# Attention interleaved with a squared-ReLU layer: batch 1's projection, its attention steps and the copy of V moved in the schedule, one more square on ScalarE

## Chip, cores, metric

The kernel runs on one core of one Trainium2 chip. The metric is device time in microseconds, the median of several executions of the whole kernel; lower is better. "Batch 0", "batch 1" and so on are the eight items of the batch; the change's "second batch" is batch 1.

TensorE is PE in the profile, its weight loads PEld, VectorE is DVE, ScalarE is ACT, GpSimd is POOL, SyncE is SP. A profile line names what an instruction writes and, after the arrow, what it reads: Q_sb, K_sb and V_sb are the loaded inputs, ps_kv the projection, qT and kT the transposed Q and K, vp the projected V, ps_att what attention computes on TensorE, h_relu and hsq the relu and its square. L462 is line 462 of the run's own kernel, so one instruction can have different lines in two kernels.

## The reference, cut

```python
# q, k, v: (8 batches, 8 heads, 1024 rows, 64); E, F: (64, 1024); w_in: (512, 2048); w_out: (2048, 512)
k_proj = einsum('ks,bhsd->bhkd', E, k)          # 64 projected rows per head
v_proj = einsum('ks,bhsd->bhkd', F, v)
attn   = softmax(q @ k_proj^T / 8)              # only 64 columns
x      = (attn @ v_proj) reordered to (8192, 512)
h      = maximum(x @ w_in, 0)
out    = (h * h) @ w_out
```

## The kernel before

The squared-ReLU layers keep TensorE busy. While batch b runs through them, the attention of batch b+1 is put between their matmuls. A batch's layers are a list of small steps: 16 steps of the first layer and 15 of the second, for each of two chunks (in batch 0 both first layers come before both second layers). The second layer is computed from sums and differences of blocks, tiles s (of the squares) and T (of the weights), which VectorE makes; its results are ps_x, ps_y and ps_z. Tables say which attention call comes before which step. On TensorE, VectorE and ScalarE the instructions keep the order in which the Python code emits them; on SyncE and GpSimd, which issue the DMAs, the framework chooses the order itself.

```python
def project(self):                    # 16 matmuls: K to the lower 64 partitions, V to the upper
    ps = self.ps["kv"] = ffn_psum("ps_kv")
    ...
def copy_kp(self):
    ...
    nc.vector.tensor_copy(self.kp[:, :, 0, :], ps_k)
    nc.vector.tensor_copy(self.kp[:, :, 1, :], self.kp[:, :, 0, :])
    nc.sync.dma_start_transpose(out=self.kT[:], in_=self.kp[:]...)          # K's transpose
def transpose_q(self):
    nc.sync.dma_start_transpose(out=self.qT[:], in_=self.Q[:]...)           # Q's transpose
def copy_vp(self):
    ...
    for e in range(2):
        nc.scalar.copy(self.vp[KP:P, :, e], ps_v[:, :, e])
    nc.vector.tensor_copy(self.vp[0:KP], self.vp[KP:P])                     # down to the lower partitions

BATCH_1 = {                            # calls for batch 1, between the steps of batch 0
    33: "project", 34: "copy_kp, copy_vp, transpose_q",
    45: "scores 0, scores 1, exponentials 0", 46: "exponentials 1", ... }
BATCH_2 = {**PIECES, 1: "", 2: "", 9: "project", 10: "copy_kp", 11: "copy_vp"}   # batch 2, in batch 1
ON_SCALAR = {(0, 1): (2, 4, 6), (1, 0): (4,)}    # (batch, chunk): which squares run on ScalarE

def square(k, n, ps):                  # after each first-layer step; two steps make one square
    nc.scalar.activation(r[:, n], ps[:], AF.Relu)
    ...                                # k in ON_SCALAR: nc.scalar.activation(o, r[:], AF.Square)
    nc.vector.tensor_tensor(out=o, in0=r[:], in1=r[:], op=ALU.mult)
```

Q, K and V of a batch are loaded by GpSimd into single buffers, in the order Q, K, V from batch 2 on. The load of batch 2's Q needs the buffer that batch 1's Q leaves when its transpose has been done; K and V are queued behind it.

The softmax here doesn't subtract the row's maximum and nothing guards it: scores larger than these inputs give would overflow.

Of the kernel before, what the change touches and what calls it, by code (L numbers as in the profile page):

```python
# [17 lines left out]
def kernel(  # L18
# [137 lines left out]
    class Attention:  # L156
# [30 lines left out]
        def copy_vp(self):  # L187
            self.vp = proj_pool.tile([P, H, 2, D // 2], BF16, name="vp")
            ps = self.ps["kv"]
            ps_v = ps[KP:P, :].rearrange("k (h d e) -> k h e d", h=H, e=2)  # L190
            for e in range(2):
                nc.scalar.copy(self.vp[KP:P, :, e], ps_v[:, :, e])
            nc.vector.tensor_copy(self.vp[0:KP], self.vp[KP:P])

        def scores(self, pr):
# [204 lines left out]


    PIECES = {
        0: "transpose_q", 1: "copy_kp", 2: "copy_vp",
        24: "scores 0, scores 1, exponentials 0", 25: "exponentials 1",
        27: "sums 0, values 0 0, reciprocals 0", 30: "values 0 1", 31: "normalize 0 0", 32: "normalize 0 1",
        47: "scores 2, scores 3, exponentials 2", 48: "exponentials 3",
        50: "sums 1, values 1 0, reciprocals 1", 53: "values 1 1", 54: "normalize 1 0", 55: "normalize 1 1",
    }
    BATCH_1 = {
        33: "project", 34: "copy_kp, copy_vp, transpose_q",  # L410
        45: "scores 0, scores 1, exponentials 0", 46: "exponentials 1",
        48: "sums 0, values 0 0, reciprocals 0", 51: "values 0 1, normalize 0 0", 52: "normalize 0 1",
        53: "scores 2, scores 3, exponentials 2", 54: "exponentials 3",
        56: "sums 1, values 1 0, reciprocals 1", 59: "values 1 1, normalize 1 0", 60: "normalize 1 1",
    }

    BATCH_2 = {**PIECES, 1: "", 2: "", 9: "project", 10: "copy_kp", 11: "copy_vp"}
    SECOND_HALF = {
        1: "last_of_first", 6: "second_half 0", 8: "second_half 1", 11: "second_half 2",
        12: "second_half 3, second_half 4, second_half 5",  # L420
# [2 lines left out]
        25: "T1 0", 26: "T1 1", 28: "T2 0", 30: "T2 1", 34: "T3 0", 35: "T3 1", 38: "T4 0", 39: "T4 1",  # L423
    }

    ON_SCALAR = {(0, 1): (2, 4, 6), (1, 0): (4,)}

    OPERANDS = {
        17: (0, 0, 0), 18: (0, 0, 1), 19: (0, 1, 0), 20: (0, 1, 1), 21: (0, 3, 0), 23: (0, 3, 1),
# [4 lines left out]
    def calls(table, n):  # L434
        for c in filter(None, table.get(n, "").split(", ")):
            name, *args = c.split()
            yield name, [int(a) for a in args]

    def ffn_groups(b, xT):
# [28 lines left out]
        def chunk(ch):  # L468
# [17 lines left out]
            def square(k, n, ps):  # L486
# [8 lines left out]
                o = hsq[:, :, j, :] if h != h1 else hsq[:, h, j:j + 2, :]  # L495
                if k in ON_SCALAR.get((b, ch), ()):
                    nc.scalar.activation(o, r[:], AF.Square)
# [160 lines left out]
    with tc.manual_schedule(engines=ORDERED):  # L658
# [10 lines left out]
        for b in range(B):  # L669
            for n, g in enumerate(ffn_groups(b, cur.xT)):  # L670
# [7 lines left out]
                if nxt:  # L678
                    for name, args in calls((BATCH_1, BATCH_2, PIECES)[min(b, 2)], n):
                        getattr(nxt, name)(*args)  # L680
# [36 lines left out]
```

## Time and profile before

| | before |
|---|---|
| median of 3 runs | 488.95 us (488.53 to 489.87) |
| span of the profiled run | 487.1 us, granted clock 1.0 |
| TensorE busy | 472.4 us (97%) |
| projection of batch 1 and second layers of batch 0 | 31.44 us (52.93 to 84.37) |
| batch 1, first chunk | 30.91 us (84.37 to 115.28) |
| batch 2, first chunk, for comparison | 27.88 us, without a projection (1.85 us) |

The stretches are differences of start times in the timeline of TensorE; "second layers" means here from step 32 on, whether its first work is the projection or the layer.

From the profile's page, the engines' busy time and the chain that ended last (shares of the span):

```profile
PE 472.4 (97%) x3618; PEld 292.5 (60%) x3619; DVE 317.2 (65%) x383; ACT 259.9 (53%) x408; POOL 33.0 (7%) x45
...
PE 92%; DVE 3%; ACT 2%; DMA 2%; issue 0%; SPq 0%
```

TensorE is nearly always busy, and the chain runs through it. The Trainium skill ("Perfetto Trace Analysis", section Identifying the Most-Contended Engine) says that this busy time is a bad measure of how close a kernel is to its limit. So one looks for TensorE's waits, not at its share. Those of the stretch that the change touches (line, released by, us in total, times, longest):

```profile
PE ps_att L199 <- DMA kT<-kp: 1.2, 1, 1.2
PE ps_y L462 <- DVE hsq L499: 0.7, 1, 0.7
```

The first is the wait of batch 1's scores for the transposed K. SyncE's timeline (start, duration, line, tile) and the chain from 61 to 67 us show what stands before it:

```profile
57.73 4.94 SPq L167 DMA_TRANSPOSE qT<-Q_sb  x1
62.73 1.28 SPq L185 DMA_TRANSPOSE kT<-kp  x1
```

```profile
61.18 1.50 SPq L167
62.68 0.06 issue
62.73 3.96 DMA kT<-kp
66.69 0.04 issue
66.73 0.63 PE ps_att L199 x8
```

Q's transpose was issued first, the moment Q had landed (57.7), and kept SyncE for 4.94 us. K's transpose came after it and landed at 66.69; the scores started at 66.73. The second wait is that of the second layer for the last square of batch 1's first chunk. VectorE's timeline shows its work until then (in brackets: idle before, and what ended it; the sums on line 456 between the squares, about 0.7 us each, are left out):

```profile
98.11 0.29 DVE L193 COPY vp<-vp 64x512 bf16<-64x512 bf16 x1 [2.80 <-ACT vp L192]
98.73 1.23 DVE L499 TENSOR_TENSOR hsq<-h_relu 128x1024 bf16<-128x1024 f32 x1 [0.33 <-ACT h_relu L491]
100.48 1.22 DVE L499 TENSOR_TENSOR hsq<-h_relu 128x1024 bf16<-128x1024 f32 x1
102.21 1.22 DVE L499 TENSOR_TENSOR hsq<-h_relu 128x1024 bf16<-128x1024 f32 x1
```

### The profile page before, as it was taken

Reading aid. Unit: us, or ns where it says so; the run is one execution under the profiler, and the core shown is the slowest. Engines: PE = TensorE matmul, PEld = TensorE weight load, DVE = VectorE, ACT = ScalarE, POOL = GpSimd, SP = SyncE. Lnnn points to the kernel's source line nnn. Section 1 sums busy time; section 2 is a strip of 40 time slices with the busy share of each in tenths; the row PEclk is TensorE's granted clock in tenths of the full one; section 3 lists DMA queues with packets and bytes.
Section 4 is the critical chain, followed back from the end, with each engine's and each line's share of the span. In section 5 each row is a group of like instructions: output and inputs, shape, how many; then the busy total and the mean of one; then the engine's idle time right before and its main releaser. Section 6 shows DMA issues by size and latency. Waiting matters only on the chain.

```text
span 487.1 us, 8385 instructions
## 1 busy us (share of the span) xinstructions
PE 472.4 (97%) x3618; PEld 292.5 (60%) x3619; DVE 317.2 (65%) x383; ACT 259.9 (53%) x408; POOL 33.0 (7%) x45
## 2 busy tenths in 40 slices
PE   4899999999999999999999999999999999999997
PEld 2544667465574755757466664747557484666656
DVE  2459855565947569385665848567684856848383
ACT  1387544655727556355654467365572746635351
POOL 7330020100020000200010000200000000000000
PEclk9999999999999999999999999999999999999999
DMA  9999989996289224991149920794232102020202
GB/s 163 204 205 208 161 138 218 235 188 163 38 139 227 40 87 88 149 208 41 46 87 180 176 87 12 132 212 90 88 68 72 46 1 87 2 87 0 87 0 87
DMA packets 72485, 55.46 MB, mean 114 GB/s; under 512 B 33920, under 2 KB 64640, under 8 KB 72448
## 3 DMA queue, kind: packets, MB, share of 16 engines
q0 software_dynamic: 30320, 29.36, 38.3%
q1 hardware_dynamic: 42128, 25.56, 20.5%
q8 instruction: 28, 0.46, 0.4%
q14 instruction: 9, 0.07, 0.0%
HBM read 59.24 MB, written 16.78 MB: 156 GB/s over the span
## 4 chain that ended last, share of the span: by engine, by line
PE 92%; DVE 3%; ACT 2%; DMA 2%; issue 0%; SPq 0%
PE ps_h L442 43%; PE ps_y L462 23%; PE ps_z L462 11%; PE ps_x L462 5%; PE ps_kv L175 3%; PE ps_att L214 2%; PE ps_att L199 2%; DVE hsq L499 1%; DMA kT<-kp 1%; DMA e_f<-in_E_dram 1%; ACT h_relu L491 1%; PE ps_k L249 1%; PE ps_fill L341 0%; ACT expT L302 0%; DVE qT L287 0%
## 5 line engine op out<-in xcount | busy, mean ns | idle before, releaser
L442 PE MATMUL ps_h<-xT,w_in 128*128 128x512 bf16 x1024 | 224.8, 379 | 0.0
L499 DVE TENSOR_TENSOR hsq<-h_relu 128x1024 bf16<-128x1024 f32 x124 | 151.2, 1222 | 63.0 <-ACT h_relu L491 63.0
L491 ACT ACTIVATE h_relu<-ps_h 128x512 f32<-128x512 f32 x256 | 150.9, 597 | 65.5 <-PE ps_h L442 65.3
L442 PEld LDWEIGHTS <-w_in 128*128 128x128 bf16 x1024 | 99.6, 98 | 117.9 <-issue 2.0
L462 PEld LDWEIGHTS <-s 128*128 128x128 bf16 x1024 | 98.5, 98 | 19.5 <-issue 8.1
L462 PEld LDWEIGHTS <-hsq 128*128 128x128 bf16 x768 | 73.2, 98 | 19.9 <-DVE hsq L499 3.4
L462 PE MATMUL ps_y<-T,s 128*128 128x256 bf16 x512 | 62.2, 273 | 0.1
L568 DVE TENSOR_TENSOR o_sb<-ps_z,p_b 128x512 f32<-128x512 f32 x16 | 11.1, 692 | 53.5 <-issue 25.7
L456 DVE TENSOR_TENSOR s<-hsq 128x1024 bf16<-128x1024 bf16 x64 | 43.6, 684 | 0.0
L564 ACT COPY o_sb<-ps_y 128x512 f32<-128x512 f32 x15 | 8.8, 585 | 56.3 <-PE ps_y L462 56.1
L233 DVE TENSOR_TENSOR xT<-ps_att,rs 128x1024 bf16<-128x1024 f32 x28 | 33.0, 1217 | 6.9 <-ACT rs L227 6.9
L462 PE MATMUL ps_y<-w_out,hsq 128*128 128x256 bf16 x256 | 34.4, 273 | 0.7 <-DVE hsq L499 0.7
L462 PE MATMUL ps_x<-w_out,hsq 128*128 128x256 bf16 x256 | 33.2, 273 | 0.0
L462 PE MATMUL ps_y<-T,hsq 128*128 128x256 bf16 x256 | 31.6, 272 | 0.0
L462 PE MATMUL ps_z<-w_out,s 128*128 128x256 bf16 x256 | 30.8, 273 | 0.0
L462 PE MATMUL ps_z<-T,s 128*128 128x256 bf16 x256 | 30.7, 273 | 0.0
L206 ACT ACTIVATE expT<-ps_att 128x1024 bf16<-128x1024 f32 x28 | 27.2, 1028 | 5.4 <-PE ps_att L199 5.4
L564 ACT COPY p_b<-ps_y 128x512 f32<-128x512 f32 (+1 forms) x17 | 9.5, 560 | 27.9 <-PE ps_y L462 27.8
L78 POOL DMA_DIRECT2D Q_sb<-in_q_dram x7 | 6.1, 876 | 265.1 <-DMA qT<-Q_sb 264.7
L568 DVE TENSOR_TENSOR o_sb<-ps_y,p_d 128x512 f32<-128x512 f32 (+1 forms) x17 | 11.2, 660 | 18.5 <-PE ps_y L462 18.5
L456 DVE TENSOR_TENSOR s<-s,hsq 128x1024 bf16<-128x1024 bf16 x32 | 21.9, 687 | 0.5
L226 ACT ACTIVATE rs<-ps_att 128x1024 f32<-128x1024 f32 x14 | 14.3, 1023 | 14.7 <-PE ps_att L214 14.7
(73 smaller groups left out, 237.7 us busy)
## 6 DMA issues: line engine op xcount, KB each, us to landing
out_dram<-o_sb SPq DMA_DIRECT2D x30, 512.0 KB, 2.9
K_sb<-in_k_dram POOLq DMA_DIRECT2D x7, 1024.0 KB, 17.2
V_sb<-in_v_dram POOLq DMA_DIRECT2D x7, 1024.0 KB, 22.6
Q_sb<-in_q_dram POOLq DMA_DIRECT2D x7, 1024.0 KB, 10.0
w_in<-in_moe_w_in_dram POOLq DMA_DIRECT2D x8, 256.0 KB, 14.1
w_out<-in_moe_w_out_dram POOLq DMA_DIRECT2D x4, 512.0 KB, 14.4
K_sb<-in_k_dram POOLq DMA_DIRECT2D x2, 512.0 KB, 8.0
Q_sb<-in_q_dram POOLq DMA_DIRECT2D x2, 512.0 KB, 13.1
```

Source lines behind the costliest of these rows:

```text
L175: nc.tensor.matmul(ps[0:KP, :], lhsT=ET[:, i, :], rhs=kv[:, :, i, :], start=f, stop=l)
L199: nc.tensor.matmul(ps[o, bank, :], lhsT=self.kT[r, 2 * pr + j, :], start=True, stop=True, rhs=self.qT[r, NT * (2 * pr + j):NT * (2 * pr + ...
L206: nc.scalar.activation(e[:], self.ps["s", pr][:], AF.Exp, scale=SCALE)
L226: nc.scalar.activation(rs[:], self.ps["r", g][:], AF.Ln)
L233: nc.vector.tensor_tensor(out=self.xT[:, 2 * g + e].rearrange("p a n t -> p a (n t)"), in0=self.ps["v", g, e][:], in1=self.rs[g][:], op=AL ...
L442: nc.tensor.matmul(ps[:], lhsT=w_in_blk(cb, fb), rhs=xT[:, cb, :, 2 * ch:2 * ch + 2], start=(cb == 0), stop=(cb == NCB - 1),)
L456: nc.vector.tensor_tensor(out=s[o][:, js], in0=x, in1=y, op=op)
L462: nc.tensor.matmul(ps[tb] if len(ps) == 2 else ps[0][:, tb], lhsT=lhs[:, j, tb * P:(tb + 1) * P], rhs=rhs[:, j], start=first and n == 0 an ...
L491: nc.scalar.activation(r[:, n], ps[:], AF.Relu)
L499: multiply = lambda: nc.vector.tensor_tensor(out=o, in0=r[:], in1=r[:], op=ALU.mult)
L564: nc.scalar.copy(to[:, t], ps)
L568: nc.vector.tensor_tensor(out=to[:, t], in0=ps, in1=more[:, t], op=ALU.add)
```

## The change

Its intent: have batch 1's projected K copied and transposed sooner, ahead of Q; take the copy of V to the lower partitions out of VectorE's way; give ScalarE a second square in batch 1's first chunk. Batch 1's scores, exponentials, sums and values also move one step (about 0.87 us) later, the projection one step earlier; two of the four normalizations keep their step.

```diff
             for e in range(2):
                 nc.scalar.copy(self.vp[KP:P, :, e], ps_v[:, :, e])
+
+        def copy_v_down(self):
             nc.vector.tensor_copy(self.vp[0:KP], self.vp[KP:P])
 ...
-        0: "transpose_q", 1: "copy_kp", 2: "copy_vp",
+        0: "transpose_q", 1: "copy_kp", 2: "copy_vp", 4: "copy_v_down",
 ...
     BATCH_1 = {
-        33: "project", 34: "copy_kp, copy_vp, transpose_q",
-        45: "scores 0, scores 1, exponentials 0", 46: "exponentials 1",
-        48: "sums 0, values 0 0, reciprocals 0", 51: "values 0 1, normalize 0 0", 52: "normalize 0 1",
-        53: "scores 2, scores 3, exponentials 2", 54: "exponentials 3",
-        56: "sums 1, values 1 0, reciprocals 1", 59: "values 1 1, normalize 1 0", 60: "normalize 1 1",
+        32: "project", 33: "copy_kp, transpose_q, copy_vp", 36: "copy_v_down",
+        46: "scores 0, scores 1, exponentials 0", 47: "exponentials 1",
+        49: "sums 0, values 0 0, reciprocals 0", 52: "normalize 0 0, values 0 1", 53: "normalize 0 1",
+        54: "scores 2, scores 3, exponentials 2", 55: "exponentials 3",
+        57: "sums 1, values 1 0, reciprocals 1", 59: "normalize 1 0", 60: "values 1 1, normalize 1 1",
     }
-    BATCH_2 = {**PIECES, 1: "", 2: "", 9: "project", 10: "copy_kp", 11: "copy_vp"}
+    BATCH_2 = {**PIECES, 1: "", 2: "", 4: "", 9: "project", 10: "copy_kp", 11: "copy_vp", 14: "copy_v_down"}
 ...
-    ON_SCALAR = {(0, 1): (2, 4, 6), (1, 0): (4,)}
+    ON_SCALAR = {(0, 1): (2, 4, 6), (1, 0): (4, 6)}
```

## The prediction

> **What bounds the kernel now.** The profile's first part gives TensorE (PE) 472.4 of 487.1 us, 97%, at granted clock 1.0; the chain of waits is 92% PE. The Trainium skill ("Perfetto Trace Analysis", section Identifying the Most-Contended Engine) warns that matmul busy time is a poor measure of headroom; here the timeline shows 64 back-to-back 512-column matmuls in 13.81 us, 216 ns each, so in steady state the work itself limits. The change can only win back stalls of PE, and batches 2, 3 and 4 (57.60 us each, first layer to first layer) have none. It touches the join to batch 1, and batch 1.
>
> Stalls in reach (waits of PE, timeline of PE):
> 1. At 65.5 us batch 1's scores wait 1.20 us, put down to kT. The timeline of SP shows Q's transpose issued first (57.73, when Q lands; issue 4.94 us, landed 66.33), then kT's (62.73, landed 66.69).
> 2. Batch 1's first chunk lasts 30.91 us against batch 2's 27.88. Of these 3.03 us, 1.85 are projection matmuls; 1.2 are lost, 0.7 in a wait for the last square (until 103.49).
>
> **What the change does.** No bytes or matmuls are added or removed.
> - Projection one step earlier (about 52.9 us); V lands at about 52.6, so it just fits. kp is copied by about 56.9, so kT's transpose (issue 1.28 us) can go before Q's. Scores move one step (0.87 us) later, to about 66.4. Q's transpose is issued at about 58.2 and should land at 65.7 to 66.8, without kT beside it. The skill ("DMA: Bandwidth & Descriptors", section Queues, rings and completion order) says that each DMA engine consumes a queue's descriptors in ring order; the trace agrees so far as kT lands 0.36 us after Q. Gain 0.7 to 1.2.
> - Given back: exponentials 1 now follow a 0.58 us PSUM copy on ScalarE that waits for PE, so sums may wait 0.1 to 0.3 us, twice. And batch 2's loads start when Q's transpose has landed; its V lands at about 92.0 (issue 68.6 plus 23.4), only 0.3 us before its projection. PE arriving 1 us earlier waits there unless the transpose lands earlier too: about 0.3 lost.
> - Copy of V down (0.29 us): VectorE sat idle 2.80 us before it in batch 1, but the next square waits anyway for a relu that ends at 98.7. About nothing by itself.
> - Square of step 6 to ScalarE (1.06 us for 1.22 on VectorE). VectorE is late from 98.7 to 106 and loses a square, but ScalarE delays the last relu from 101.0 to about 101.8. The last square ends near 103.1 instead of 103.44: gain 0.3, range 0 to 0.8.
>
> **Sum.** -0.9 (stall 1) +0.5 (given back) -0.4 (stall 2) is -0.8 us. Predicted 488.1 us, range 486.9 to 489.1. At most 2.4 us (0.5%) is reachable: faster 1%, same 98%, slower 1%.
>
> **What would show each step.** Timeline of SP: kT's issue near 57, before Q's. Waits of PE: the 1.20 us on kT gone or below 0.5, then named after Q's transpose. A new PE wait for V's load at batch 2's projection (about 91.5). Batch 1's first chunk about 30.5 us, its wait for the last square about 0.4. Later batches still 57.60.
>
> **What would make it wrong.** SP still issuing Q's transpose first: then no gain at stall 1 beyond the later step's 0.87 us. V of batch 1 landing late under the earlier projection. PSUM buffers given out differently. If neither hand-back occurs and stall 2 vanishes, 486.6.

## The result

488.18 us, median of 3 runs (487.98 to 488.58), against 488.95; ratio 0.9982, 95% interval 0.9958 to 1.0007. By the 2% rule: the same. Five more runs in another session gave 488.39 against 489.23, ratio 0.9983 (0.9971 to 0.9996), so a gain of about 0.8 us is there. A ratio is the mean time of one kernel's runs over that of the other's of the same rounds, so it is not quite the ratio of the medians quoted.

The same views of the changed kernel. The page:

```profile
PE 473.3 (97%) x3619; PEld 292.6 (60%) x3619; DVE 316.1 (65%) x382; ACT 260.9 (54%) x409; POOL 32.9 (7%) x45
...
PE 94%; ACT 2%; DVE 2%; DMA 1%; issue 0%
```

TensorE's waits from 50 to 120 us:

```profile
PE ps_y L464 <- DVE hsq L501: 0.3, 1, 0.3
```

The wait for kT is gone from the list and the one for the last square has fallen from 0.7 to 0.3 us. SyncE's timeline, though, is not what the change's words or the prediction say:

```profile
57.57 4.92 SPq L167 DMA_TRANSPOSE qT<-Q_sb  x1
62.54 1.27 SPq L185 DMA_TRANSPOSE kT<-kp  x1
```

Q's transpose is still issued first. VectorE's timeline shows the second copy of K before it:

```profile
57.13 0.28 DVE L183 COPY kp<-kp 64x512 bf16<-64x512 bf16 x1
```

K had been copied by 57.41, 0.16 us before, and K's transpose nevertheless waited behind Q's, as in the kernel before. It landed at about 66.84 (issue 62.54 plus 4.3 us to landing), so no sooner than before. What helped is on TensorE: the step put in between and then the scores, which came to where they are at 67.11, after the landing:

```profile
66.14 1.03 PE L464 MATMUL ps_y<-T,hsq 128*128 128x256 bf16 x8
67.11 0.63 PE L201 MATMUL ps_att<-qT,kT 64*64 64x512 bf16 x8
67.66 0.50 PE L464 MATMUL ps_y<-T,hsq 128*128 128x256 bf16 x3
```

VectorE before the last square of batch 1's first chunk (sums left out again):

```profile
98.29 1.23 DVE L501 TENSOR_TENSOR hsq<-h_relu 128x1024 bf16<-128x1024 f32 x1 [3.46 <-ACT h_relu L493]
100.74 0.29 DVE L195 COPY vp<-vp 64x512 bf16<-64x512 bf16 x1
101.33 1.23 DVE L501 TENSOR_TENSOR hsq<-h_relu 128x1024 bf16<-128x1024 f32 x1 [0.30 <-ACT h_relu L493]
```

One square fewer stands there and the last one starts at 101.33 instead of 102.21. The stretches, with a second profile of each kernel (the second of before is a single run, state unknown):

| profile | first PE work | batch 0, second layers from | batch 1 from | stretch | first chunk of batch 1 | batch 2 from |
|---|---|---|---|---|---|---|
| before | 5.08 | 52.93 | 84.37 | 31.44 | 30.91 | 145.00 |
| before, again | 5.58 | 53.80 | 84.56 | 30.76 | 30.90 | 145.19 |
| changed | 5.58 | 53.61 | 83.87 | 30.26 | 30.53 | 144.13 |
| changed, again | 5.58 | 53.76 | 84.02 | 30.26 | 30.47 | 144.22 |

By the means of these pairs, batch 1 starts 0.52 us earlier and its first chunk takes 0.40 us less: 0.92 us together, as batch 2's start shows (145.10 against 144.18). The runs' medians gave 0.77 and 0.84.

### The profile page after: what moved, and what is told of

Read it like the earlier page. It is cut to its first block, busy times and chain, and to the rows that moved or that the text cites. A ratio compares the mean times of both kernels' runs of the same rounds, so it can differ in the third digit from the quotient of the medians.

```text
span 486.2 us, 8385 instructions
## 1 busy us (share of the span) xinstructions
PE 473.3 (97%) x3619; PEld 292.6 (60%) x3619; DVE 316.1 (65%) x382; ACT 260.9 (54%) x409; POOL 32.9 (7%) x45
## 4 chain that ended last, share of the span: by engine, by line
PE 94%; ACT 2%; DVE 2%; DMA 1%; issue 0%
PE ps_h L444 44%; PE ps_y L464 24%; PE ps_z L464 11%; PE ps_x L464 6%; PE ps_kv L175 3%; PE ps_att L216 2%; PE ps_att L201 2%; ACT h_relu L493 1%; DVE hsq L501 1%; DMA e_f<-in_E_dram 1%; PE ps_fill L343 1%; PE ps_k L251 1%; DVE qT L289 1%; PE ps_v L273 0%; PE ps_att L310 0%
```

## Experiments

Theory A, formed on the result: of all that was moved, two things gain. The later scores hide a landing of kT that itself does not move, and the square on ScalarE shortens VectorE's late chain. A second landing, of batch 2's V at about 92 us, stands close behind. Rivals are named in each expectation. Times are medians; the kernel before ran in the same sessions (489.23 us in the first, 489.17 in the second, 489.33 in the third).

### The changed kernel again, and the kernel before again

No edit. Changed kernel:

> The changed kernel once more, for its spread. Theory A: two DMA landings bound it, which do not depend on when TensorE arrives: batch 1's transposed K at about 66.8 us and batch 2's V at about 91.9 us of the profile. If this profile starts as early as the one of before (first transposes on TensorE at 5.1 us instead of 5.6), the scores wait 0.3 to 0.4 us for kT and batch 2's projection up to 0.6 us for V; after batch 2's projection both profiles lie within 0.2 us of each other. Rival B: the later start of the changed profile (0.5 us) belongs to the change and is seen again here. Time 488.2, ratio to before 0.998 to 0.999. Wait for the last square 0.26 us again.

Measured: 488.39 us (0.9983, given above); start at 5.58 again, waits for neither kT nor V, 0.3 us for the last square. The kernel before, one look:

> The kernel before once more, for a second profile. Every kernel profiled since starts its first TensorE transposes at 5.6 us or later, only the first profile of before at 5.1. If the start varies from run to run (theory A), this one is not bound to 5.1; if it starts at 5.6, the wait for kT is about 0.7 us instead of 1.2 (as in the kernel with the early projection only), since kT's landing at 66.7 to 67.1 does not move with it, and batch 1's first layer begins at 84.4 to 84.7 us all the same. If it starts at 5.1 again (rival B), the wait is 1.2 us and the later start belongs to the changed kernels.

Measured: 489.07 us, start at 5.58, waits of TensorE:

```profile
PE ps_y L462 <- DVE hsq L499: 0.7, 1, 0.7
PE ps_att L199 <- DMA kT<-kp: 0.5, 1, 0.5
```

So the later start does not belong to the change. Nor does the early start alone explain the 1.20 us: e6b, e8 and e9 below also start at 5.12 to 5.14, but reach step 32 at 53.38 to 53.67, while the first profile of before was there at 52.93, earlier than all 13 others (53.37 to 54.73). And the wait for kT is 0.5 us when TensorE comes 0.9 us later to the second layer, though batch 1 then starts at nearly the same time, 84.56 against 84.37. That is what a landing does that does not depend on TensorE: it swallows whatever TensorE was ahead. **The 1.20 us on which the prediction was built came from one profile in which TensorE came unusually early**; 0.5 us is the value in the second profile, and e3 and e7 below, which up to there change nothing but the place of a short VectorE copy (e7), have 0.4 us.

### Only the later step (e1)

```diff
-        45: "scores 0, scores 1, exponentials 0", 46: "exponentials 1",
+        46: "scores 0, scores 1, exponentials 0", 47: "exponentials 1",
 ...            (all of BATCH_1 from here on as in the changed kernel; project stays at 33)
```

> The kernel before with batch 1's attention steps one step later and nothing else. Theory A (the later step alone hides the wait for kT, since kT still lands after Q's transpose at about 66.7): wait for kT 0 to 0.4 us instead of 1.20, from the start of batch 0's second layer (first ps_y) to batch 1's first layer 30.3 to 30.7 us instead of 31.44; wait for the last square still 0.7 us; V of batch 2 may be waited for, up to 0.6 us. Time about 488.4 to 488.7. Rival (the earlier projection and copies are what removes the wait): the wait stays 1.2 us less 0.87, but sums and normalization lose it again, time 489.

Measured: 488.61 us (0.9991, 0.9979 to 1.0004). The interval includes 1, so the reading rests on the profile. TensorE's waits from 50 to 120 us are down to the last square's, 0.7 as before:

```profile
PE ps_y L462 <- DVE hsq L499: 0.7, 1, 0.7
```

No wait for kT; stretch 30.36 us, almost the changed kernel's 30.26. The first chunk became 31.29 us, and the timeline of TensorE shows why:

```profile
91.68 0.40 PE L175 MATMUL ps_kv<-K_sb,ET 128*64 128x512 bf16 x1
92.09 0.38 PE L176 MATMUL ps_kv<-V_sb,FT 128*64 128x512 bf16 x1
92.09 0.40 PE L175 MATMUL ps_kv<-K_sb,ET 128*64 128x512 bf16 x1
```

The first projection matmul on K starts at 91.68, the first on V at 92.09; in undisturbed runs the two start within 0.01 us. TensorE had to wait 0.4 us for batch 2's V. So the later step alone does what the change does at the scores, and the landing of V took part of it back.

### Only the earlier projection (e2)

```diff
-        33: "project", 34: "copy_kp, copy_vp, transpose_q",
+        32: "project", 33: "copy_kp, transpose_q, copy_vp",
```

> The kernel before with only the projection, the copies of K and the transposes one step earlier; scores stay at step 45. Theory A: SP still issues Q's transpose first, when Q has landed at 57.6, and kT's after it at 62.5; kT lands at 66.7 to 66.9 and the scores wait 1.2 us as before; time as before within 0.2 us. Rival (earlier copies help): kT lands up to 1 us earlier, wait 0.2 to 0.4 us, time 488.2.

Measured: 489.19 us (1.0001, 0.9987 to 1.0015). Q's transpose first (57.67), K's at 62.69, and the wait for kT is still there:

```profile
PE ps_att L199 <- DMA kT<-kp: 0.7, 1, 0.7
```

I had expected 1.2 us. TensorE came to step 32 at 53.83; the kernel before, which came at 53.80 in its second profile, waited 0.5 us. Batch 1 from 84.71, not sooner than before (84.37 and 84.56). The earlier projection and copies gain nothing.

All profiles together say the same. The five without the later step (before twice, e2, e3, e7) wait 0.4 to 1.2 us for kT, and their stretches are 30.61 to 31.44 us. The seven with the later step and Q's transpose first (changed twice, e1, e4, e5, e8, e9) do not wait for it: 30.26 to 30.36 us.

### K's transpose really first (e6)

A copy of two columns of Q onto themselves, placed after the copies of K, makes Q's transpose depend on VectorE, so that K's transpose is issued first. The result stays correct.

```diff
+        def touch_q(self):
+            nc.vector.tensor_copy(self.Q[:, 0, 0:2], self.Q[:, 0, 0:2])
 ...
-        32: "project", 33: "copy_kp, transpose_q, copy_vp", 36: "copy_v_down",
+        32: "project", 33: "copy_kp, touch_q, transpose_q, copy_vp", 36: "copy_v_down",
```

> The changed kernel with a copy of two columns of Q onto themselves on VectorE after the copies of K, on which Q's transpose then depends, so that SP issues K's transpose first: the order that the change's words and my prediction assumed. The prediction's premise: kT issued at 57.5 and landed by 62, Q's transpose issued at about 58.8 and landed at 65.7 to 66.8; wait at the scores 0 to 0.3 us, now for Q's transpose. Rival (the two transposes take the same time together in either order): the later of the two lands at 66.8 as before, nothing gained. Batch 2's V lands 25 to 26 us after Q's transpose has landed, so it moves with it; V in batch 2 is waited for 0 to 0.7 us. Time 488.0 to 488.4.

Measured: 499.7 us (1.022, 1.0203 to 1.0236): 10 us slower than before, which neither theory expected. SyncE:

```profile
58.83 1.67 SPq L188 DMA_TRANSPOSE kT<-kp  x1
60.63 14.97 SPq L170 DMA_TRANSPOSE qT<-Q_sb  x1
```

The order is as wanted, but the issue of Q's transpose took 14.97 us instead of 4.92, it landed 17.1 us after its start, and TensorE waited:

```profile
PE ps_att L204 <- DMA qT<-Q_sb: 9.5, 1, 9.5
```

GpSimd's timeline names the suspect. The edit had also changed the order in which the framework queued batch 2's loads: K and V now came before Q, so that they no longer stood behind a load that waits for Q's transpose, and they started just before it:

```profile
56.94 0.87 POOL L78 DMA_DIRECT2D K_sb<-in_k_dram  x1 [24.22 <-PE ps_kv L179]
57.81 0.88 POOL L78 DMA_DIRECT2D V_sb<-in_v_dram  x1
78.25 0.87 POOL L78 DMA_DIRECT2D Q_sb<-in_q_dram  x1 [19.56 <-DMA qT<-Q_sb]
```

After the wait TensorE was slow for a while (stretch, its length; busy time and count of PE, PEld, DVE, ACT and POOL; then the granted clock, here 0.50 and 0.60; DMA share and GB/s):

```profile
77.80:80.00 2.20, 2.17 (x14) 1.08 (x15) 0.00 (x0) 1.02 (x1) 0.87 (x1) 0.50 0.24 84
80.00:84.00 4.00, 4.00 (x36) 2.64 (x34) 0.00 (x0) 1.51 (x2) 0.00 (x0) 0.60 1.02 134
```

The skill ("TensorE: Matmul & The Clock Gate", Part 1: The HAM clock gate) says that the array falls back to half its clock after an idle window of about 3.4 us; this run agrees, with 0.50 after a wait of 9.5 us, and it is the only one here in which TensorE, once started, waits so long.

### K's transpose first, with the loads held back (e6b)

To part the order from the loads: as e6, but two small VectorE instructions that read the transposed Q together with K and V keep batch 2's loads of K and V back until that transpose has landed, and the loads are called for later.

```diff
+        def hold_loads(self, before):
+            junk = soft_pool.tile([P, 2], BF16, tag="junk", name="junk", bufs=1)
+            for t in (before.K, before.V):
+                nc.vector.tensor_tensor(out=junk[:], in0=self.qT[:, 0, 0:2], in1=t[:, 0, 0:2], op=ALU.add)
 ...
+                    if b == 0 and n == 46:
+                        nxt.hold_loads(nxt)
 ...
-                    if n == (35, 12, 1)[min(b, 2)]:
+                    if n == (46, 12, 1)[min(b, 2)]:
```

> K's transpose issued before Q's as in e6, but batch 2's loads are held until Q's transpose has landed (a small VectorE read of qT, K and V), which e6 lost: there K and V of batch 2 were loaded beside Q's transpose, whose issue took 14.97 us. Theory: those loads, not the order, cost the 9.5 us. Then the issue takes about 5 us again, Q's transpose lands at 65.5 to 67.0, the wait at the scores is 0 to 0.5 us and the time 488.0 to 489.0. Rival: the order itself is slow (K's transpose of 64 partitions ahead of Q's), then the wait stays near 9 us and the time near 499.

Measured: 488.45 us (0.9986, 0.9973 to 1.0000).

```profile
57.23 1.31 SPq L193 DMA_TRANSPOSE kT<-kp  x1
58.67 5.26 SPq L175 DMA_TRANSPOSE qT<-Q_sb  x1
```

```profile
PE ps_att L209 <- DMA qT<-Q_sb: 0.3, 1, 0.3
```

The issue takes 5.26 us again and the 9.5 us are gone, so the loads beside the transpose were their cause, not the order. The skill ("DMA: Bandwidth & Descriptors", section Issuing engines are not separate DMA queues) says that DMAs of SyncE and GpSimd run on the same 16 DMA engines and interleave; these two runs agree, with 14.97 and 5.26 us. The same shows at batch 2's transpose of Q. In all profiles but e6 it is issued while K and V are still being loaded, and its issue takes 12.3 to 15.4 us (4.72 to 4.75 us in batches 4 to 7 of before). In e6 V had landed at 74.7, long before, and it takes 4.72 us. The first profile of before, then e6:

```profile
79.69 12.88 SPq L167 DMA_TRANSPOSE qT<-Q_sb  x1
89.81 4.72 SPq L170 DMA_TRANSPOSE qT<-Q_sb  x1
```

The intended order as such gains nothing. kT lands at about 60.8 (57.23 plus 3.6), but Q's transpose then at about 67.2 (58.67 plus 8.5), and the scores need both. The later of the two lands at 67.2 in e6b, and with Q first at 66.2 to 67.3 in all profiles but one (e5, where everything was late, 68.0).

### Only the square on ScalarE (e3)

```diff
-    ON_SCALAR = {(0, 1): (2, 4, 6), (1, 0): (4,)}
+    ON_SCALAR = {(0, 1): (2, 4, 6), (1, 0): (4, 6)}
```

> The kernel before with the square of step 6 of batch 1 on ScalarE and nothing else. Theory (from the prediction: one square fewer on the late VectorE, one more on ScalarE): wait for the last square 0.2 to 0.4 us instead of 0.70, batch 1's first chunk 30.4 to 30.6 us instead of 30.9; the wait for kT stays, 0.5 us with the usual start at 5.6 and up to 1.2 with a start at 5.1. Time 0.3 to 0.5 us below before. Rival (the square gains nothing, the moved copy of V does): chunk 30.9.

Measured: 488.79 us (0.9985, 0.9968 to 1.0002), wait for the last square 0.3 us, first chunk 30.47 us, wait for kT 0.4 us. The 0.4 us of the first chunk belong to the square.

### Only the later copy of V (e7)

```diff
+        def copy_v_down(self):
             nc.vector.tensor_copy(self.vp[0:KP], self.vp[KP:P])
 ...    (called at 4 in PIECES, at 36 in BATCH_1, at 14 in BATCH_2; nothing else moves)
```

> The kernel before with only the copy of V to the lower partitions moved some steps later. The prediction said about nothing. Theory now: VectorE was waiting anyway where the copy stood (until 98.1 us), but where it goes, between the squares of steps 6 and 7, VectorE has work without a gap, so the copy's 0.29 us is added to the late chain: wait for the last square 0.9 to 1.1 us instead of 0.70, first chunk 31.1 to 31.3 us, time 0.2 to 0.3 us above before. Rival (waiting for ScalarE was what made VectorE late): wait below 0.7, chunk below 30.9.

Measured: 489.95 us (1.0006, 0.9985 to 1.0027), first chunk 31.33 us, wait for the last square:

```profile
PE ps_y L464 <- DVE hsq L501: 1.1, 1, 1.1
```

By itself this part costs 0.42 us in the first chunk (31.33 against 30.91). VectorE's idle time before the copy, 2.80 us, had cost nothing, since the next square waited for a relu until 98.7 anyway. At step 14 the copy stands between squares of a busy VectorE. In the changed kernel the square that went to ScalarE leaves it room there: with both moves the first chunk takes 30.53 and 30.47 us, with the square's alone (e3) 30.47.

### Batch 2's projection one step earlier (e5)

```diff
-    BATCH_2 = {..., 9: "project", 10: "copy_kp", 11: "copy_vp", 14: "copy_v_down"}
+    BATCH_2 = {..., 8: "project", 9: "copy_kp", 10: "copy_vp", 13: "copy_v_down"}
```

> The changed kernel with batch 2's projection one step (0.87 us) earlier. Theory A: TensorE comes to it at 90.9 to 91.1 us and V lands at 90 to 92.1 (it landed between those bounds in the runs so far, with the landing of Q's transpose of batch 1), so it waits 0 to 1.2 us, most likely 0.5 to 0.9 in the profile; time about 0.3 to 0.9 us above the changed kernel, 488.7 to 489.2. Rival (V's landing does not bind): no wait for V, first chunk 30.5, same time as the changed kernel.

Measured: 489.93 us (1.0004, 0.9983 to 1.0024), first chunk 32.55 us, and

```profile
PE ps_kv L176 <- DMA V_sb<-in_v_dram: 1.7, 1, 1.7
```

The wait is there and larger than expected: V landed at 94.0 (issue 69.90 plus 24.1), outside the bounds that I had given. Batch 1's Q had landed late in this run, the slowest of the six (490.91 us): its transpose was issued at 59.08, against 57.3 to 58.1 in the others with Q first. Issue and time to landing give 91.8 us for V in both profiles of the changed kernel, 92.0 and 91.7 in those of before, 90.9 and 91.1 in e3 and e7, and 92.5 in e9 below. So V's landing does not follow TensorE, which came to this projection at 92.83 and 92.95 in e3 and e7, later than in the changed kernel, and the changed kernel has almost no slack to it: its projection began at 91.82 and 91.97 us, in the first of them with V's part 0.09 us after K's.

### Batch 2's projection one step later (e4), with V's copy behind the relus (e8), without the square (e9)

```diff
-    BATCH_2 = {..., 9: "project", 10: "copy_kp", 11: "copy_vp", 14: "copy_v_down"}
+    BATCH_2 = {..., 10: "project", 11: "copy_kp", 12: "copy_vp", 15: "copy_v_down"}     # e4, e9
+    BATCH_2 = {..., 10: "project", 11: "copy_kp", 16: "copy_vp", 17: "copy_v_down"}     # e8
-    ON_SCALAR = {(0, 1): (2, 4, 6), (1, 0): (4, 6)}
+    ON_SCALAR = {(0, 1): (2, 4, 6), (1, 0): (4,)}                                       # e9 only
```

> The changed kernel with batch 2's projection, and the copies of K and V behind it, one step (0.87 us) later. Theory A (batch 2's V lands at 91.9 to 92.1 us, and TensorE waits for it when it comes sooner): no wait for V any more in any execution; in the profile the gain is as large as the wait of the changed kernel's profile, 0 to 0.1 us, and up to 0.5 us in executions that start early; batch 1's first chunk 30.4 to 30.5 us. Time 487.8 to 488.2, so 0.1 to 0.4 us less than the changed kernel's 488.39 in the same session. Rival (V's landing costs nothing): same time as the changed kernel.

> As e4, and the copies of projected V on ScalarE in batch 1 move behind the chunk's last relu (step 16), the copy down to step 17. Theory: in the changed kernel the last square waits for ScalarE, whose 0.64 us of copies of V sit before the last five relus; without them the last relu ends when TensorE's last group is done plus 0.6 us, and the wait of 0.26 us for the last square goes. First chunk of batch 1 30.0 to 30.2 us instead of 30.47 to 30.53. Time 0.2 to 0.4 us below e4. Rival (VectorE's own queue makes the square late): wait stays 0.2 us or more.

> As e4 (batch 2's projection at step 10), but the square of step 6 stays on VectorE. Theory: with the projection one step later, the relu and square of step 4 run on ScalarE under the projection, and VectorE can start the square of step 5 some 1.5 us earlier relative to the second layer, so the move of the square is not needed: wait for the last square 0 to 0.1 us, first chunk 30.1 to 30.3 us, time as e4, 487.6 to 488.0. Rival (the square's move is what made e4 fast): wait 0.3 to 0.7 us, chunk 30.5 to 30.9, time 488.1 or more.

Measured, e4 and e8 in one session, e9 in the next:

| | time | ratio to before (interval) | first chunk | wait for the last square |
|---|---|---|---|---|
| e4 | 487.69 us | 0.9967 (0.9954 to 0.9981) | 30.16 us | none listed |
| e8 | 487.61 us | 0.9971 (0.9959 to 0.9984) | 30.08 us | none listed |
| e9 | 487.65 us | 0.9964 (0.9945 to 0.9983) | 30.24 us | none listed |

For e4 I had expected the first chunk to stay at 30.4 to 30.5 us; the one step took the last square's wait away as well. ScalarE in e4 shows how:

```profile
92.02 0.60 ACT L493 ACTIVATE h_relu<-ps_h 128x512 f32<-128x512 f32 x1 [0.27 <-PE ps_h L444]
92.88 0.60 ACT L493 ACTIVATE h_relu<-ps_h 128x512 f32<-128x512 f32 x1 [0.27 <-PE ps_h L444]
93.51 1.06 ACT L499 ACTIVATE hsq<-h_relu 128x1024 bf16<-128x1024 f32 x1
95.70 0.60 ACT L493 ACTIVATE h_relu<-ps_h 128x512 f32<-128x512 f32 x1 [1.13 <-PE ps_h L444]
96.56 0.60 ACT L493 ACTIVATE h_relu<-ps_h 128x512 f32<-128x512 f32 x1 [0.27 <-PE ps_h L444]
97.84 0.60 ACT L493 ACTIVATE h_relu<-ps_h 128x512 f32<-128x512 f32 x1
```

With the projection one step later, the second relu of step pair 4 and its square (93.51) run while TensorE is in the projection, and the following relus keep up with TensorE; the square of pair 5 starts on VectorE at 97.19, against 98.29 in the changed kernel. e9 shows that the square's move to ScalarE is then not needed, and e8's further move of V's copies brought nothing that the times can show, so that its expectation of 0.2 to 0.4 us below e4 failed. All three beat the kernel before with intervals clear of 1, though by the 2% rule they too are the same. None of the three is shown to be the best; e9 has the fewest edits. Its profile has no slack to V either: the projection began at 92.52, just as V landed. In e4 V landed at 91.6 and the projection began at 92.77. That they also beat the changed kernel rests on medians of different sessions (487.6 to 487.7 against 488.39), whose intervals overlap, and on the first chunk in the profiles (30.08 to 30.24 against 30.47 to 30.53).

## Why the prediction was right, and where it was not

The sum was right: 488.1 us predicted, 488.18 measured, both changes of 0.8 us, all inside the join of batches and batch 1. That it fits so closely is partly luck, for its parts held less well.

- **Bound by TensorE, little in reach: right.** From batch 2's start to the end of the span the first profiles of both kernels take 342.1 us (487.1 less 145.00, 486.2 less 144.13), and the untouched second chunk of batch 1 takes 29.72 and 29.73 us.
- **"kT's transpose (issue 1.28 us) can go before Q's": wrong.** SyncE issued Q's first, as before. Where this went wrong: I read the order from the change, although the trace of before already showed Q's transpose ahead of K's where the code had K's first. The prediction had named this as what could make it wrong, and said that no more than the later step's 0.87 us would then be gained; that is what happened. e6b shows that the right order would have gained nothing.
- **"Gain 0.7 to 1.2" at the scores: the mechanism was the later step, and the size was off.** e1 and e2 show that the later step does it and the earlier projection does not. The term was sized by a wait of 1.20 us in a profile in which TensorE came early; the second profile of before has 0.5 us, and batch 1 starts 0.52 us earlier in the mean of the pairs.
- **"Given back" 0.5 us: mostly not seen.** The sums did not wait in the changed profile: exponentials 1 ended at 70.26 and the sums started at 70.39, with no wait listed. A wait for V was at most 0.09 us there, though e1 shows 0.4 us and e5 1.72 us of it. The two errors, 0.9 for about 0.5 gained and 0.5 for about 0 given back, cancelled. How much the unprofiled runs of the changed kernel wait for V stays open: no trace shows them.
- **Square on ScalarE, gain 0.3: right** (0.44 alone in e3, 30.91 to 30.47 against a predicted chunk of about 30.5; wait 0.3 against 0.4). The mechanism held too: the last relu ended at 101.29 and the last square at 102.56, in a profile in which batch 1 started 0.50 us earlier; with that added back they are at 101.8 and 103.1, as predicted.
- **Copy of V "about nothing by itself": wrong**, it costs 0.42 us alone (e7). I priced the place that it left and not the place where it went.

Each part was profiled once (the changed kernel and the one before twice), and the intervals of e1, e2, e3 and e7 include 1: what each part does is read from the waits and stretches, not from whole runs.

## What to carry to other kernels

Read from the trace whether a wait ends with work that your change moves, or with a DMA landing that it does not move: in the second case putting the consumer later hides it, and getting there sooner only meets the next landing. Take the size of such a wait from more than one profile, for it shrinks by whatever the waiting engine came late. When an instruction is moved, price the place where it goes, and check on the DMA-issuing engines which order was really built, for a dependency added for one transfer can let quite another start beside it.

## What the Trainium skill lacked or had wrong

- "DMA: Bandwidth & Descriptors", section Rules for kernel authors: it says that a transpose next to ordinary DMAs needs nothing, which is about correct data. That a transpose can be slow there is not stated: the issue of the same transpose took 14.97 us with K's and V's loads in flight (e6) and 5.26 us without (e6b), and landed after 17.1 and 8.5 us.
- The same page, section Queues, rings and completion order: descriptors of one queue are consumed in ring order on each engine. The landings are consistent with it, and nothing is shown to be wrong: issued second, kT landed about 0.4 us after Q's transpose in the first profile of before (up to 2.5 us after it in the others with Q first); issued first, about 6.3 us before it (e6b). Landings alone do not show the order within an engine.
- No page that I read gives the scatter from one execution to the next: the first TensorE work began at 5.08 to 5.92 us in these profiles, TensorE came to step 32 at 52.93 to 54.73, and one wait behind it measured 1.20 or 0.5 us in the same kernel. What causes the scatter was not looked into.
